# Products of the gradient one unit later in a sliding-window attention backward, and projections in other PSUM banks

## The chip, the cores and the metric

One core of a Trainium2 chip runs one program that computes a forward pass and all its gradients. The metric is the device time of one execution in microseconds (us). The five engines each work through a list of their own in the order in which the program wrote it: TensorE (PE, matrix products and transposes, its weight loads shown as PEld), VectorE (DVE), ScalarE (ACT), GpSimd (POOL) and SyncE (SP), which here only issues DMA transfers. They wait for each other through semaphores.

## The reference

S = 2048 rows, D = 512, 32 heads of Dh = 16, a window of W = 256 keys, F = 1376. Two branches are mixed by a gate per row; the outputs are the mix and the gradients of `A_x`, of both weights of the attention, of the three weights of the feed-forward part and of `gate_w`.

```python
qkv = (x @ wqkv).reshape(B, S, 3, H, Dh).transpose(2, 0, 3, 1, 4)
scores = einsum("bhqd,bhkd->bhqk", q, k) * Dh ** -0.5      # keys 0..255 behind the query only
p = softmax(scores); a = (p @ v).reshape(B, S, D) @ wo
gate = x @ W_gate; up = x @ W_up; b = (gate * (gate > 0) * up) @ W_down
g = sigmoid((x * gate_w).sum(-1, keepdims=True))
out = g * a + (1 - g) * b                                  # and its vjp with grad_out
```

Both branches read the same x, `A_x`.

## The kernel before

There are three stages. **The first** (about 0 to 250 us) computes the feed-forward hidden layer and its gradients in 44 steps, one per block of 128 hidden columns and group of 512 rows; a loop over step numbers `n` (lines 439 to 498) runs eight steps longer than there are steps, so that the delayed parts come out, and in those last steps it also makes the projections of the attention's first group. **The second** (about 250 to 720 us) is the attention, forward and backward, and is where the change lies. **The third** (to the end) reads the spilled gradients back and computes the output and `dx`.

The attention is written as 360 *units*. A unit is one block of 128 queries against one block of 128 keys, for four heads: `c` (0 to 3) is a set of eight heads, `j` (0 to 15) the query block, `kb` = j, j-1 or j-2 the key block (roles "d" for diagonal, "m" for middle, "f" for far), `half` which four of the eight heads. A query block with its full window thus has six units. The while loop from line 875 writes one *slot* per unit, with the parts of several units in it; which part of which unit falls in which slot sets the order of work on every engine. In slot n:

- `front` of unit n (line 666): the scores ST on TensorE (line 672), their exponential on ScalarE (line 682), and for roles d and f the mask on GpSimd (lines 684, 687);
- `gradp` of unit n-1 (line 698): VectorE multiplies the exponentials Pu by the product dPT, which gives Pd. This is "the product" below;
- `flip` of unit n-2 by a DMA transpose, for units that are turned that way;
- `rowsum` of unit n-3 (line 703, `LAG` = 3): four pairs of small matmuls into the bank BA, the first of a pair with Pu (line 710), the second with Pd (line 712). Units of role f, and some of role m, are then turned by eight transposes on TensorE into a bank `pt` and copied out by ScalarE and VectorE in turn (line 734);
- `front_dp` of unit n (line 690): dPT, the gradient of the probabilities, on TensorE (line 696). In the first slot after a finished query block it stands ahead of `rowsum`;
- then pieces that fill the slot: CD (lines 533, 536), the gradients of keys and values; one *part* of the projections of the next group of four query blocks (`project_parts`, line 118); or a quarter of a weight gradient (`grad_parts`, line 613), whose tile is held over four such pieces. A planner counts a `credit` of TensorE time per slot to decide, with a due time per group.

A group (c, four query blocks) has six parts, in order: Q and dO (a matmul chain of four, an evacuation to zT by VectorE), the DMA transpose `tr_rows`, K and V (a matmul chain of four, an evacuation KT or VT by ScalarE, then two masked copies K0, K1 or V0, V1 by VectorE, line 161), and `tr_kv` (eight transposes, two copies on VectorE). After Q and dO of group g+1, four copies called `spread` on VectorE (line 514), one a slot, put them in place.

PSUM has eight banks. In this stage four have the tag M and take ST, dPT, the projections' pp and the weight gradients' wps; two have the tag TR and take the transposes pt and ptp; one is BA, one CD. A tile that finds no free bank of its tag waits for the reader of the one that it is given.

Of the kernel before, what the change touches and what calls it, by code (L numbers as in the profile page):

```python
# [11 lines left out]
BF = mybir.dt.bfloat16  # L12
F32 = mybir.dt.float32
# [9 lines left out]
def kernel(  # L23
# [20 lines left out]
    nc = tc.nc  # L44
    P = 128
# [10 lines left out]
    DC = D // P  # L56
# [55 lines left out]
    if True:  # L112
        HH = HG // 2
        proj = {}
        groups = [(c, tg) for c in range(DC) for tg in range(NTG)]
        PENG = ("dvs", "dvs")

        def project_parts(c, tg):
            t4 = {}
            proj[(c, tg)] = t4  # L120
            pj = pjA if (c * NTG + tg) % 3 == 0 else pjs["b"]

            def mm(nm, which, eng):
                ps, tag, bufs, _, _ = pools["now"]
                pp = ps.tile([P, TGW], F32, tag=tag, bufs=bufs, name="pp")
                for cd in range(DC):
                    if which < 3:
                        nc.tensor.matmul(pp[:], lhsT=w_p[c][:, cd, which * P:(which + 1) * P], rhs=x_T[tg][:, cd, :],  # L128
                                         start=(cd == 0), stop=(cd == DC - 1))
                    else:  # L130
                        nc.tensor.matmul(pp[:], lhsT=w_p[c][:, cd, 3 * P:4 * P], rhs=da_T[tg][:, cd, :],
                                         start=(cd == 0), stop=(cd == DC - 1))
                if nm in ("Q", "dO"):
                    if nm == "Q":
                        t4["z"] = pjA.tile([P, 2, TGW], BF, tag="zT", name="zT")
                    dst = t4["z"][:, ("Q", "dO").index(nm), :]
                else:
                    dst = pjA.tile([P, TGW], BF, tag="T", bufs=2, name=f"{nm}T")[:]
                if nm == "Q" and (c, tg) == groups[1]:
                    nc.scalar.mul(dst, pp[:], scale)  # L140
                elif nm == "Q":
                    nc.vector.tensor_scalar(dst, pp[:], scale, None, op0=ALU.mult)
                else:
                    evac(dst, pp[:], eng)
                t4[nm] = dst
                if nm in ("Q", "dO"):
                    if c == 0 and tg == 0:
                        w = ("Q", "dO").index(nm)
                        for k in range(NP):
                            rows = slice(32 * k, 32 * k + 32)  # L150
                            evac(zt[0][rows, w, k, :, :], dst[rows, :].rearrange("p (k q) -> p k q", k=TPG),
                                 (("dve", "act")[w] if k % 2 else "dve"))
                else:
                    for k in range(2):
                        t4[f"{nm}{k}"] = pj.tile([P, TGW], BF, tag=f"{nm}{k}", name=f"{nm}{k}")
                        if PENG[k] == "act":
                            nc.scalar.mul(t4[f"{nm}{k}"][:], pp[:], par[:, k:k + 1])
                        elif PENG[k] == "dve":
                            nc.vector.tensor_scalar(t4[f"{nm}{k}"][:], pp[:], par[:, k:k + 1], None, op0=ALU.mult)
                        else:  # L160
                            nc.vector.tensor_scalar(t4[f"{nm}{k}"][:], dst[:], par[:, k:k + 1], None, op0=ALU.mult)

            def tr(a_nm, b_nm):
                _, _, _, ps, trt = pools["now"]
                pt = ps.tile([P, 2, TPG, P], BF, tag=trt, bufs=2, name="ptp")
                for a, nm in enumerate((a_nm, b_nm)):
                    for k in range(TPG):
                        nc.tensor.transpose(pt[:, a, k, :], t4[nm][:, k * P:(k + 1) * P], ident[:])
                return pt

            def tr_rows():
                rows = pjA.tile([P, 2, TPG, P], BF, tag="rows", bufs=2, name="rows")
                nc.sync.dma_start_transpose(out=rows[:].rearrange("p a t d -> p (a t) d"),
                                            in_=t4["z"][:].rearrange("p a s -> p (a s)"))
                t4["rows"] = rows

            def tr_kv():
                kv = pj.tile([P, TPG, HG, 34], BF, tag="KV1", name="KV1")
                nc.gpsimd.memset(kv[:, :, :, 0:1], -1.0)
                nc.gpsimd.memset(kv[:, :, :, Dh + 1:Dh + 2], 1.0)  # L180
                pt = tr("K", "V")
                v = lambda a: pt[:, a, :, :].rearrange("p k (h d) -> p k h d", h=HG)
                nc.vector.tensor_scalar(kv[:, :, :, 1:1 + Dh], v(0), scale, None, op0=ALU.mult)
                nc.vector.tensor_copy(kv[:, :, :, Dh + 2:2 * Dh + 2], v(1))
                t4["kv"] = kv

            return [lambda: mm("Q", 0, "dve"), lambda: mm("dO", 3, "dve"), tr_rows, lambda: mm("K", 1, "act"),
                    lambda: mm("V", 2, "act"), tr_kv]

    with ExitStack() as p1, tc.manual_schedule():  # L190
# [248 lines left out]
        for n in range(N1 + 8):  # L439
# [51 lines left out]
            for _ in range({N1 + 1: 2, N1 + 2: 0}.get(n, 1)):  # L491
                if first:
                    first.pop(0)()
            z = n - DA0 - NT - 2
            if z == 0:
                load_w(0)
# [4 lines left out]
    if True:  # L501
# [6 lines left out]
        ps = pps.enter_context(tc.tile_pool(name="attps", bufs=2, space=PSUM))  # L508
        ppr = ExitStack()
        psr = ppr.enter_context(tc.tile_pool(name="attpr", bufs=2, space=PSUM, side="right"))  # L510
        pools["now"] = (ps, "M", 4, psr, "TR")
        def spread(gi, k):
            rows = slice(32 * k, 32 * k + 32)
            nc.vector.tensor_copy(zt[gi % ZB][rows, :, k, :, :].rearrange("p w t q -> p w (t q)"),
                                  proj[groups[gi]]["z"][rows, :, :])

        P2 = {}
        RQ = {}
        CDs = {}
# [93 lines left out]
        def grad_parts(c, tail=False):  # L613
# [6 lines left out]

            def piece(part, t0, first, last):
                if first:
                    hold[part] = ps.tile([P, 3, P], F32, tag="M", bufs=4, name="wps")
                wps = hold[part]
                for t in range(t0, t0 + 4):
                    nc.tensor.matmul(wps[:], lhsT=x_r[:, t, part * P:(part + 1) * P], rhs=sts[c][:, t, 0:3, :],  # L626
                                     start=first and t == t0, stop=last and t == t0 + 3)
                if not last:
                    return None
                ws = (S2["t6"] if tail else gwp).tile([P, 3, P], BF, tag="ws", bufs=5 if tail else 2, name="ws")  # L630
                evac(ws[:], wps[:], "act" if not tail or part % 2 else "dve")
                return store(part, ws)
# [33 lines left out]
        def front(u):  # L666
# [5 lines left out]
            nc.tensor.matmul(ST[:], lhsT=KTt[:, ksl], rhs=z[:, 0, :, jl, :], start=True, stop=True)  # L672
            if not u.own:
                if u.half == 0:
                    kind = "m" if u.c == DC - 1 and u.j > 11 and u.j % 2 == 0 else u.role
                    tag = f"PP{kind}"
                    pairs[(u.c, u.j, u.kb)] = wk.tile([P, 2, 2, HH, P], BF, tag=tag, bufs=3, name=tag)
                u.PP = pairs[(u.c, u.j, u.kb)][:, u.half, :, :, :]
# [42 lines left out]
        def flip(u):  # L721
# [3 lines left out]
            if u.dma:  # L725
# [5 lines left out]
                for b in range(2)[hs]:  # L731
                    P2[(u.c, u.j, u.kb, b)] = P2[key][:, b, :, :, :]
                return
            eng = ("act", "dve")[copier["i"] % 2]
            copier["i"] += 1
            pt = psr.tile([P, 2, HH, P], BF, tag="TR", name="pt")
            for a, src in enumerate((u.Pu, u.Pd)):
# [99 lines left out]
        with tc.manual_schedule():  # L837
# [37 lines left out]
            while n <= NU + LAG or ev or cdq or bgq:  # L875
                now = ev.pop(n, [])
                u = units[n] if n < NU else None
                if u is not None:
# [2 lines left out]
                        sts[u.c] = st.tile([P, NT, 4, P], BF, tag="rows_st", name="rows_st")  # L881
                    if u.first and u.j % TPG == 0:
                        if gi + 1 < len(groups):
                            prq = project_parts(*groups[gi + 1])
                            due = n + sum(2 * min(3, j + 1) for j in range(u.j, u.j + TPG)) - 3
                            if gi + 2 == len(groups):
                                due -= 10
# [9 lines left out]
                for eng, f in now:  # L897
                    if eng == "pool":
                        f()
                if 1 <= n <= NU:  # L900
                    gradp(units[n - 1])
                for eng, f in now:
                    if eng == "dve":
                        f()
                for eng, f in now:
                    if eng == "pool+":
                        f()
                if 2 <= n < NU + 2 and units[n - 2].dma:
                    flip(units[n - 2])
                w = units[n - LAG] if LAG <= n < NU + LAG else None  # L910
                if u is not None and w is not None and w.first:
                    front_dp(u)
                    pieces()
                if w is not None:
                    rowsum(w)
# [2 lines left out]
                    if w.last:  # L918
# [5 lines left out]
                        for kb in done:  # L924
                            qbs = range(kb, min(NT, kb + 3))
                            for qb in qbs:
                                for half in range(2):
                                    e = n + (1 if qb < w.j else 5)
                                    cdq.append((e, w.c, kb, qb, half, qb == qbs[-1] and half == 1))
                if u is not None and not (w is not None and w.first):  # L930
                    front_dp(u)
                credit += SLOT - 0.63 - (0.44 if LAG <= n < NU + LAG and not units[n - LAG].dma else 0.0)
                if not (u is not None and w is not None and w.first):
                    pieces()
                if n >= NU:
                    if bgq:
# [23 lines left out]
                if late and (u is None or u.c == 0 or (n % 12 == 1 and 3 <= u.j <= 8 if u.c < DC - 1 else  # L960
                                                       n % 4 == 1 and 1 < u.j < 10 or n % 2 and u.j > 9)):
                    late.pop(0)()
                if early and n % 3 == 0 and (len(early) > 4 or u is None or u.j >= 11):
                    early.pop(0)()
                credit = max(-1.0, min(1.2, credit))
                for eng, f in now:
# [154 lines left out]
```

## Time and profile before

| what | value |
|---|---|
| median of three runs | 921.34 us (919.93 to 921.94) |
| profiled execution: its own time, its span | 921.62 us, 919.9 us |
| granted TensorE clock, mean | 0.998 |
| TensorE busy | 903.5 us, 98% |
| VectorE, ScalarE, GpSimd busy | 511.5, 437.8, 493.6 us |
| from 270 to 720 us (450 us): TensorE, VectorE, ScalarE, GpSimd busy | 443.37, 341.60, 320.82, 325.55 us |
| scores ST, dPT, products on VectorE | 360 each |

Times of lines are in us from the start of the span. A row of the timeline gives start, duration, engine, line, operation and tiles, and in brackets the idle time of the engine before it and what ended it. Rows of the same kind that follow each other are merged, with their number at the end. A matmul's end in a row is modelled and lies after the start of the next one, so TensorE's share of busy time hides gaps of up to a few tenths; they are read from starts. Records of neighbouring VectorE instructions overlap by a little under a tenth too.

### The profile page before, as it was taken

How to read it: one execution, taken by the hardware profiler on the slowest of the kernel's cores; microseconds unless marked ns; L12 is line 12 of the kernel's file. 1: busy time of each engine (PE TensorE's matmuls, PEld its weight loads, DVE VectorE, ACT ScalarE, POOL GpSimd, SP SyncE). 2: the span in 40 equal slices, each digit the busy share in tenths (PEclk: the TensorE clock that was granted, in tenths of full speed). 3: DMA queues.
4: the chain of work that ended last, by engine and by line, in shares of the span. 5: the costliest groups of instructions: out<-in, count | busy, mean ns of one | idle time of the engine just before them, and what ended most of it. 6: DMA issues, size and time to landing. Idle time of an engine off the chain costs nothing.

```text
span 919.9 us, 26221 instructions
## 1 busy us (share of the span) xinstructions
PE 903.5 (98%) x10711; PEld 569.7 (62%) x10711; DVE 511.5 (56%) x957; ACT 437.8 (48%) x773; POOL 493.6 (54%) x937
## 2 busy tenths in 40 slices
PE   9999999999999999999999999999998999999998
PEld 6556656556657776667666677766776644444445
DVE  4333344334288887668876687777786222222223
ACT  7322222222367777667776677766687300011111
POOL 4544445445277777767787677775777311111111
PEclk9999999999999999999999999999999999999999
DMA  9988889999699999998999989999999799777741
GB/s 303 193 195 188 190 179 215 221 222 194 159 164 157 179 182 187 191 164 149 171 196 187 162 158 182 184 179 185 181 187 197 184 255 234 183 188 184 184 93 46
DMA packets 505576, 169.07 MB, mean 184 GB/s; under 512 B 433456, under 2 KB 504336, under 8 KB 505456
## 3 DMA queue, kind: packets, MB, share of 16 engines
q1 hardware_dynamic: 484816, 145.51, 85.8%
q10 hardware_dynamic: 19008, 17.31, 6.9%
q0 software_dynamic: 1632, 4.59, 1.4%
q8 instruction: 83, 1.36, 0.6%
q14 instruction: 37, 0.30, 0.1%
HBM read 32.28 MB, written 36.24 MB: 74 GB/s over the span
## 4 chain that ended last, share of the span: by engine, by line
PE 79%; POOL 7%; DVE 4%; DMA 4%; issue 2%; ACT 2%; SPq 1%; ACTq 0%; POOLq 0%; DVEq 0%
PE dxps L1046 8%; PE ST L672 7%; PE dPT L696 7%; PE wps L403 7%; PE pt L739 5%; PE wps L626 4%; PE dxps L1050 4%; PE bps L1019 4%; PE pp L128 4%; PE CD L533 3%; PE BA L710 3%; PE dps L405 3%; PE ups L354 3%; PE gps L354 3%; PE dhps L354 3%
## 5 line engine op out<-in xcount | busy, mean ns | idle before, releaser
L696 PE MATMUL dPT<-z,V 128*128 128x512 bf16 x360 | 136.4, 379 | 3.7 <-ACT PPm L682 2.4
L672 PE MATMUL ST<-z,K 128*128 128x512 bf16 x360 | 136.3, 379 | 2.0 <-ACT PPm L682 0.3
L684 POOL TENSOR_SCALAR_AFFINE_SELECT PPd<-PPd 128x512 bf16<-128x512 bf16 x124 | 79.1, 638 | 106.9 <-ACT PPd L682 106.1
L701 DVE TENSOR_TENSOR Pd<-Pu,dPT 128x512 bf16<-128x512 bf16 x117 | 80.1, 684 | 64.7 <-POOL Pu L687 62.7
L368 POOL TENSOR_TENSOR hT<-rg,upm 128x512 bf16<-128x512 bf16 x44 | 51.5, 1171 | 116.1 <-DVE upm L366 90.0
L403 PE MATMUL wps<-dgu_r,x_r 128*128 128x256 bf16 (+1 forms) x704 | 103.9, 270 | 0.9 <-DVE wst L74 0.8
L701 DVE TENSOR_TENSOR PPd<-PPd,dPT 128x512 bf16<-128x512 bf16 x124 | 84.4, 680 | 15.5 <-POOL PPd L684 14.8
L403 PEld LDWEIGHTS <-x_r 128*128 128x128 bf16 x704 | 68.3, 98 | 31.9 <-issue 1.8
L682 ACT ACTIVATE PPd<-ST 128x512 bf16<-128x512 f32 x124 | 74.4, 600 | 27.3 <-PE ST L672 26.5
L682 ACT ACTIVATE PPm<-ST 128x512 bf16<-128x512 f32 x119 | 71.2, 601 | 29.9 <-PE ST L672 25.8
L682 ACT ACTIVATE Pu<-ST 128x512 bf16<-128x512 f32 x117 | 70.2, 600 | 28.9 <-PE ST L672 28.8
L701 DVE TENSOR_TENSOR PPm<-PPm,dPT 128x512 bf16<-128x512 bf16 x119 | 79.4, 667 | 6.5 <-POOL PPm L684 4.1
L687 POOL TENSOR_SCALAR_AFFINE_SELECT Pu<-Pu 128x512 bf16<-128x512 bf16 x112 | 73.7, 658 | 16.2 <-ACT Pu L682 15.6
L1026 ACT COPY a_sb<-aps 128x512 f32<-128x512 f32 x16 | 9.4, 586 | 151.4 <-issue 137.6
L366 DVE SCALAR_TENSOR_TENSOR upm<-rg,ups 128x512 bf16<-128x512 bf16 x44 | 30.1, 684 | 80.6 <-PE ups L354 44.2
L360 ACT ACTIVATE rg<-gps 128x512 bf16<-128x512 f32 x44 | 26.3, 598 | 88.4 <-PE gps L354 33.1
L405 PE MATMUL dps<-db_r,h_r 128*128 128x512 bf16 x176 | 66.7, 379 | 0.0
L72 ACT COPY p<-pt 128x1024 bf16<-128x1024 bf16 x62 | 63.0, 1016 | 5.2 <-PE dPT L696 0.4
L378 POOL TENSOR_TENSOR dgu<-dh_sb,rg 128x512 bf16<-128x512 bf16 x44 | 57.2, 1301 | 5.1 <-ACT dh_sb L374 5.1
L1032 POOL DMA_DIRECT2D out_dram<-o_sb x16 | 8.7, 542 | 89.2 <-DVE o_sb L1030 82.7
L128 PE MATMUL pp<-x,p 128*128 128x512 bf16 x192 | 49.0, 378 | 1.5 <-ACT PPm L682 1.0
L626 PE MATMUL wps<-rows_st,x_r 128*128 128x384 bf16 x256 | 50.3, 325 | 0.0
(193 smaller groups left out, 2362.3 us busy)
## 6 DMA issues: line engine op xcount, KB each, us to landing
dqkvo_d<-rows_st SPq DMA_DIRECT2D x15, 512.0 KB, 4.2
hT_d<-hT ACTq DMA_DIRECT2D x44, 128.0 KB, 2.5
dgT_d<-dgu ACTq DMA_DIRECT2D x44, 128.0 KB, 3.0
duT_d<-dgu ACTq DMA_DIRECT2D x44, 128.0 KB, 3.0
duT_g<-duT_d SPq DMA_DIRECT2D x8, 640.0 KB, 5.6
gt<-hT_d SPq DMA_DIRECT2D x7, 640.0 KB, 6.0
dgT_g<-dgT_d SPq DMA_DIRECT2D x7, 640.0 KB, 5.3
out_dram<-wst SPq DMA_DIRECT2D x20, 128.0 KB, 2.7
```

The lines of the kernel that those rows point to most:

```text
L128: nc.tensor.matmul(pp[:], lhsT=w_p[c][:, cd, which * P:(which + 1) * P], rhs=x_T[tg][:, cd, :], start=(cd == 0), stop=(cd == DC - 1))
L354: nc.tensor.matmul(out[:], lhsT=w(c), rhs=x(c), start=(c == 0), stop=(c == DC - 1))
L403: nc.tensor.matmul(acc["w"][:, c, 0:2 * nw], lhsT=x_r[:, t, c * P:(c + 1) * P], rhs=k.dgu_r[:, :, i, s0:P], start=(go_ and c % 2 == 0), st ...
L405: nc.tensor.matmul(acc["d"][:], lhsT=k.h_r[:, i, :], rhs=db_r[:, t, :], start=go_, stop=no_)
L626: nc.tensor.matmul(wps[:], lhsT=x_r[:, t, part * P:(part + 1) * P], rhs=sts[c][:, t, 0:3, :], start=first and t == t0, stop=last and t == ...
L672: nc.tensor.matmul(ST[:], lhsT=KTt[:, ksl], rhs=z[:, 0, :, jl, :], start=True, stop=True)
L682: nc.scalar.activation(u.Pu[:], ST[:], ACT.Exp)
L684: nc.gpsimd.affine_select(out=u.Pu[:], in_=u.Pu[:], compare_op=ALU.is_ge, fill=0.0, base=0, pattern=[[0, HH], [1, P]], channel_multiplier=-1)
L687: nc.gpsimd.affine_select(out=u.Pu[:], in_=u.Pu[:], compare_op=ALU.is_ge, fill=0.0, base=-1, pattern=[[0, HH], [-1, P]], channel_multiplier=1)
L696: nc.tensor.matmul(u.dPT[:], lhsT=VTt[:, ksl], rhs=z[:, 1, :, jl, :], start=True, stop=True)
L701: nc.vector.tensor_tensor(out=u.Pd[:], in0=u.Pu[:], in1=u.dPT[:], op=ALU.mult)
L1046: nc.tensor.matmul(to, lhsT=src[:, fc, lsl], rhs=W6[(wt, fc)][:, cols], start=(fc == 0 and wt == "Wg"), stop=False)
```

## The change

In the attention's loop, `gradp` in slot n takes unit n-2 where it took n-1, `front_dp` takes unit n-1 where it took n, and the DMA `flip` takes unit n-3 where it took n-2. `front` (unit n) and `rowsum` (unit n-3) stay where they are, as does everything else in the slot: the evacuations of parts, the `spread` copies, the CD pieces.

The projections' tiles pp move from the four M banks to the two TR banks, and so do the weight gradients' tiles wps of the head sets c = 0 and 1, which run while c = 1 and 2 are at work.

Q, dO and `tr_rows` of the second group are made in the last steps of the first stage (steps N1+4 to N1+6), in that stage's banks, with the four `spread` copies right behind dO. The attention's first group then has only K, V and `tr_kv` to make for the second.

Smaller: while c = 0, two of three TensorE-turned units are copied out by ScalarE instead of one of two. In c = 3 the diagonal units share the middle units' buffers at j = 12 only, not at 12 and 14. The transposed loads of the third stage's first group (`early`) start at other slots: the four DMAs from j = 14 on, every second slot, instead of from j = 11 on, every third.

```diff
--- before.py
+++ after.py
@@ -115,10 +115,15 @@
         groups = [(c, tg) for c in range(DC) for tg in range(NTG)]
         PENG = ("dvs", "dvs")
 
+        def spread(gi, k):
+            rows = slice(32 * k, 32 * k + 32)
+            nc.vector.tensor_copy(zt[gi % ZB][rows, :, k, :, :].rearrange("p w t q -> p w (t q)"),
+                                  proj[groups[gi]]["z"][rows, :, :])
+
         def project_parts(c, tg):
             t4 = {}
             proj[(c, tg)] = t4
-            pj = pjA if (c * NTG + tg) % 3 == 0 else pjs["b"]
+            pj = lambda: pjA if (c * NTG + tg) % 3 == 0 else pjs["b"]
 
             def mm(nm, which, eng):
                 ps, tag, bufs, _, _ = pools["now"]
@@ -150,9 +155,12 @@
                             rows = slice(32 * k, 32 * k + 32)
                             evac(zt[0][rows, w, k, :, :], dst[rows, :].rearrange("p (k q) -> p k q", k=TPG),
                                  (("dve", "act")[w] if k % 2 else "dve"))
+                    elif nm == "dO" and (c, tg) == groups[1]:
+                        for k in range(NP):
+                            spread(1, k)
                 else:
                     for k in range(2):
-                        t4[f"{nm}{k}"] = pj.tile([P, TGW], BF, tag=f"{nm}{k}", name=f"{nm}{k}")
+                        t4[f"{nm}{k}"] = pj().tile([P, TGW], BF, tag=f"{nm}{k}", name=f"{nm}{k}")
                         if PENG[k] == "act":
                             nc.scalar.mul(t4[f"{nm}{k}"][:], pp[:], par[:, k:k + 1])
                         elif PENG[k] == "dve":
@@ -175,7 +183,7 @@
                 t4["rows"] = rows
 
             def tr_kv():
-                kv = pj.tile([P, TPG, HG, 34], BF, tag="KV1", name="KV1")
+                kv = pj().tile([P, TPG, HG, 34], BF, tag="KV1", name="KV1")
                 nc.gpsimd.memset(kv[:, :, :, 0:1], -1.0)
                 nc.gpsimd.memset(kv[:, :, :, Dh + 1:Dh + 2], 1.0)
                 pt = tr("K", "V")
@@ -491,6 +499,10 @@
             for _ in range({N1 + 1: 2, N1 + 2: 0}.get(n, 1)):
                 if first:
                     first.pop(0)()
+            if n == N1 + 3:
+                second = project_parts(*groups[1])
+            if n in (N1 + 4, N1 + 5, N1 + 6):
+                second.pop(0)()
             z = n - DA0 - NT - 2
             if z == 0:
                 load_w(0)
@@ -508,12 +520,7 @@
         ps = pps.enter_context(tc.tile_pool(name="attps", bufs=2, space=PSUM))
         ppr = ExitStack()
         psr = ppr.enter_context(tc.tile_pool(name="attpr", bufs=2, space=PSUM, side="right"))
-        pools["now"] = (ps, "M", 4, psr, "TR")
-        def spread(gi, k):
-            rows = slice(32 * k, 32 * k + 32)
-            nc.vector.tensor_copy(zt[gi % ZB][rows, :, k, :, :].rearrange("p w t q -> p w (t q)"),
-                                  proj[groups[gi]]["z"][rows, :, :])
-
+        pools["now"] = (psr, "TR", 2, psr, "TR")
         P2 = {}
         RQ = {}
         CDs = {}
@@ -620,7 +627,8 @@
 
             def piece(part, t0, first, last):
                 if first:
-                    hold[part] = ps.tile([P, 3, P], F32, tag="M", bufs=4, name="wps")
+                    own, tag, bufs = (ps, "M", 4) if c + 2 >= DC else (psr, "TR", 2)
+                    hold[part] = own.tile([P, 3, P], F32, tag=tag, bufs=bufs, name="wps")
                 wps = hold[part]
                 for t in range(t0, t0 + 4):
                     nc.tensor.matmul(wps[:], lhsT=x_r[:, t, part * P:(part + 1) * P], rhs=sts[c][:, t, 0:3, :],
@@ -672,7 +680,7 @@
             nc.tensor.matmul(ST[:], lhsT=KTt[:, ksl], rhs=z[:, 0, :, jl, :], start=True, stop=True)
             if not u.own:
                 if u.half == 0:
-                    kind = "m" if u.c == DC - 1 and u.j > 11 and u.j % 2 == 0 else u.role
+                    kind = "m" if u.c == DC - 1 and u.j == 12 else u.role
                     tag = f"PP{kind}"
                     pairs[(u.c, u.j, u.kb)] = wk.tile([P, 2, 2, HH, P], BF, tag=tag, bufs=3, name=tag)
                 u.PP = pairs[(u.c, u.j, u.kb)][:, u.half, :, :, :]
@@ -731,7 +739,7 @@
                 for b in range(2)[hs]:
                     P2[(u.c, u.j, u.kb, b)] = P2[key][:, b, :, :, :]
                 return
-            eng = ("act", "dve")[copier["i"] % 2]
+            eng = ("act", "dve", "act")[copier["i"] % 3] if u.c == 0 else ("act", "dve")[copier["i"] % 2]
             copier["i"] += 1
             pt = psr.tile([P, 2, HH, P], BF, tag="TR", name="pt")
             for a, src in enumerate((u.Pu, u.Pd)):
@@ -881,7 +889,7 @@
                         sts[u.c] = st.tile([P, NT, 4, P], BF, tag="rows_st", name="rows_st")
                     if u.first and u.j % TPG == 0:
                         if gi + 1 < len(groups):
-                            prq = project_parts(*groups[gi + 1])
+                            prq = project_parts(*groups[gi + 1]) if gi else second
                             due = n + sum(2 * min(3, j + 1) for j in range(u.j, u.j + TPG)) - 3
                             if gi + 2 == len(groups):
                                 due -= 10
@@ -897,19 +905,20 @@
                 for eng, f in now:
                     if eng == "pool":
                         f()
-                if 1 <= n <= NU:
-                    gradp(units[n - 1])
+                if 2 <= n <= NU + 1:
+                    gradp(units[n - 2])
                 for eng, f in now:
                     if eng == "dve":
                         f()
                 for eng, f in now:
                     if eng == "pool+":
                         f()
-                if 2 <= n < NU + 2 and units[n - 2].dma:
-                    flip(units[n - 2])
                 w = units[n - LAG] if LAG <= n < NU + LAG else None
-                if u is not None and w is not None and w.first:
-                    front_dp(u)
+                v = units[n - 1] if 1 <= n <= NU else None
+                if w is not None and w.dma:
+                    flip(w)
+                if v is not None and w is not None and w.first:
+                    front_dp(v)
                     pieces()
                 if w is not None:
                     rowsum(w)
@@ -927,10 +936,10 @@
                                 for half in range(2):
                                     e = n + (1 if qb < w.j else 5)
                                     cdq.append((e, w.c, kb, qb, half, qb == qbs[-1] and half == 1))
-                if u is not None and not (w is not None and w.first):
-                    front_dp(u)
+                if v is not None and not (w is not None and w.first):
+                    front_dp(v)
                 credit += SLOT - 0.63 - (0.44 if LAG <= n < NU + LAG and not units[n - LAG].dma else 0.0)
-                if not (u is not None and w is not None and w.first):
+                if not (v is not None and w is not None and w.first):
                     pieces()
                 if n >= NU:
                     if bgq:
@@ -960,7 +969,7 @@
                 if late and (u is None or u.c == 0 or (n % 12 == 1 and 3 <= u.j <= 8 if u.c < DC - 1 else
                                                        n % 4 == 1 and 1 < u.j < 10 or n % 2 and u.j > 9)):
                     late.pop(0)()
-                if early and n % 3 == 0 and (len(early) > 4 or u is None or u.j >= 11):
+                if early and (u is None or n % 2 == 0 and u.j >= (9 if len(early) > 4 else 14)):
                     early.pop(0)()
                 credit = max(-1.0, min(1.2, credit))
                 for eng, f in now:
```

## The prediction

> **What bounds the kernel now.** I read the page's busy times first, then what TensorE and VectorE waited for, then the timeline where the change acts.
>
> ```profile
> PE 903.5 (98%) x10711; PEld 569.7 (62%) x10711; DVE 511.5 (56%) x957; ACT 437.8 (48%) x773; POOL 493.6 (54%) x937
> ```
> ```profile
> PE dPT L696 <- ACT PPm L682: 2.4, 1, 2.4
> ```
> ```profile
> DVE Pd L701 <- POOL Pu L687: 62.7, 81, 1.5
> DVE PPd L701 <- POOL PPd L684: 14.8, 20, 1.7
> ```
>
> TensorE is the bound, and it is nearly full. VectorE idles 77 us before products because GpSimd's masks come late, but hardly any of that reaches TensorE. As matmul ends are modelled, I measured TensorE's gaps by starts: 512 columns take 0.216 us back to back, 128 columns 0.055 us, the smallest 0.025 us; what a start is later than that is a gap. From 249 to 719 us there are 119 gaps over 0.04 us, 23.1 us together; those over 0.12 us make 18.3 us. That is all that the change can win, so the question is what new waits it makes. They show at a projection's K, here for group c=1, j=12 to 15. TensorE, ScalarE, VectorE:
>
> ```profile
> 426.59 0.38 PE L672 MATMUL ST<-z,K 128*128 128x512 bf16 x1
> ...
> 427.70 0.38 PE L672 MATMUL ST<-z,K 128*128 128x512 bf16 x1
> 427.91 0.18 PE L710 MATMUL BA<-KV,Pu 128*128 128x33 bf16 x1
> 427.94 0.17 PE L712 MATMUL BA<-KV,Pd 128*128 128x17 bf16 x1
> ```
> ```profile
> 426.79 0.59 ACT L72 CAST KT<-pp 128x512 bf16<-128x512 f32 x1 [1.03 <-PE pp L128]
> ```
> ```profile
> 425.37 0.43 DVE L514 COPY z<-zT 32x1024 bf16<-32x1024 bf16 x1
> 426.34 0.69 DVE L701 TENSOR_TENSOR Pd<-Pu,dPT 128x512 bf16<-128x512 bf16 x1 [0.53 <-POOL Pu L687]
> 427.06 0.63 DVE L514 COPY z<-zT 32x1024 bf16<-32x1024 bf16 x1
> 427.70 1.04 DVE L161 TENSOR_SCALAR K<-KT,par 128x512 bf16<-128x512 bf16 x2
> 428.66 0.67 DVE L701 TENSOR_TENSOR PPm<-PPm,dPT 128x512 bf16<-128x512 bf16 x1
> 429.26 0.67 DVE L701 TENSOR_TENSOR Pd<-Pu,dPT 128x512 bf16<-128x512 bf16 x1
> ```
>
> K's matmuls end a slot at 426.59. ScalarE copies KT until 427.38, and VectorE, in order, makes K0 and K1 until 428.74 and only then starts the next product. The matmul of BA at 427.94 needs the product that began at 426.34, ended 0.91 us before: it stands ahead of K0 and K1 in VectorE's list.
>
> **The products (the main term).** After the change, the place in VectorE's list where product k stood holds product k-1, while `rowsum` stays where it was. So the place at 428.66, behind K0 and K1, holds the product that the matmul at 427.94 waits for. If nothing else moved, it would end at 429.33, 1.39 us late. Something does move: the 0.53 us wait for the mask at 426.34 ends, K0 can start when KT is there (427.40), and the product ends at about 429.0, still 1.1 us late. The chain from the end of K's matmuls is 0.2 (latency) + 0.6 (KT) + 0.9 (K0, K1) + 0.7 (product) = 2.4 us; TensorE reaches that `rowsum` after one slot, a ST and one small matmul, 1.35 us. Before there was one more slot (1.30 us on average) to cover it.
>
> Queued behind a late product are all the products after it; behind the waiting `rowsum` on TensorE stand the flip, dPT and the next ST, so the time is lost whole. To sum it I went down VectorE's rows from 249.5 to 720 us: each starts when the one before is done (record less 0.08 us, the overlap of neighbouring records) and its input is there (the producer's time in this trace, plus TensorE's shift so far); each product is put one place later; where it ends after its BA matmul of this trace, the difference joins the shift. With the products in their own places this gives a shift of 0.01 us, so the method invents none. One place later it gives 48.8 us:
>
> - behind K0, K1: 14 places, 13.4 us; behind V0, V1: 12, 11.6 us
> - behind `tr_kv`'s two copies: 14, 8.7 us
> - behind Q's evacuation: 14, 4.0; behind dO's: 13, 4.3; behind spread alone: 8, 2.4 us
> - behind a flip's copy on VectorE: 26, 4.4 us
>
> With an overlap of 0.06 or 0.10 us it is 52.2 or 45.4 us.
>
> **What is won.** A product no longer waits for a mask of its own slot's unit, and TensorE, when it waits at `rowsum`, gives the others time; I take all gaps over 0.12 us as gone: -18.3 us. Among them is the largest, at 701.85 to 704.60, where an exponential had no buffer because the shared PPm buffers were waiting for a DMA; j=14's diagonal units now have a buffer of their own. But a gap taken out brings TensorE to the same `rowsum` earlier, and the same walk without those gaps gives 53.4 us. Net +35.1. Bounds: no gap of before goes (+48.8), or every gap over 0.04 goes (55.9 - 23.1 = +32.8). I take the middle one because most gaps over 0.12 stand at pp waiting for an M bank or behind masks, both of which the change touches.
>
> **Q and dO of group 1 moved.** Eight matmuls, 8 x 0.216 = 1.7 us of TensorE in either place: nothing. Q's copy (ScalarE, 0.60), dO's (VectorE, 0.69), four spreads (1.85) and the DMA transpose (SP 1.84) fall where ScalarE idles from 243.4 to 249.8, VectorE from 246.4 to 250.3 and SP from 243.5 to 250.3; without that cover their 0.6 and 2.5 us would delay the first exponential and the first product. Without them the walk is 0.7 us shorter in the first group: -0.7. The gaps of 250 to 268 us make 4.0 (already in the 18.3), but 1.7 us of filling work is gone there too: between -1.7 and +1.7 around my value.
>
> **Projections and wps in TR.** The waits of pp for an M bank (16 gaps after dPT, 1.7; 23 after CD, 0.7) are in the sum above. New ones: a pp or flip waits for the copy of the flip before last, at most 1.02 us (ScalarE, pt). Flips are two or four slots apart (2.6 us or more), so with two banks the older is free: 0. While one of the eight wps tiles holds a bank, a flip waits for the one two slots back: 0.44 + 0.3 + 1.02 against 2.6 us: 0, at most 0.3 for some 16 flips, 5 us. I take 0.
>
> **The small edits.** Copier at c=0: five of 28 copies move from VectorE (0.68) to ScalarE (1.02), which is busy three quarters of the time there; -1 to +1, taken as 0. DMA flips one slot later: CD is due at least one query block after all but the last; buffers PPd and PPm have three copies; 0, up to +2 at the end. The early loads leave SP at j=11 to 13 and join four Wd loads from j=14; T0 is wanted after 733, some 15 us later: 0, up to +2.
>
> **Sum** on the profiled execution, 921.62 us (span 919.9; 0.3 above the median 921.34): 921.6 + 53.4 - 18.3 - 0.7 = 956.0 us.
>
> The clock. After the 2.53 us gap at 701.85 the trace grants half the clock from 706.08 to 709.49.
>
> ```profile
> 702.00:704.00 2.00, 0.23 (x2) 0.00 (x0) 0.18 (x1) 0.05 (x1) 0.00 (x0) 1.00 0.53 142
> ...
> 706.00:708.00 2.00, 2.00 (x28) 1.45 (x25) 1.40 (x4) 1.66 (x3) 1.75 (x5) 0.52 0.91 193
> ```
>
> Gaps up to 0.6 us in 250 to 268 left it at 1.00. My waits, up to 1.4 us, lie between, nearer the latter; I add nothing and keep a rival. The Trainium skill (TensorE: Matmul & The Clock Gate, "What's actually happening") says that the clock halves after an idle window of about 3.4 us; the trace's 2.53 us gap was enough. By that rule no wait here would trip it, and the sum stays 956.0.
>
> **Rivals.**
> - *Only K and V bite.* The lateness behind the shorter evacuations is absorbed, as VectorE, no longer waiting for masks, gets ahead. For: 77 us of mask waits end. Against: the walk has taken them out already. 13.4 + 11.6 - 18.3 = +6.7, to +15.4 with `tr_kv`: 928 to 937; with smaller or larger K waits 923 to 948.
> - *Faster.* VectorE's list is not what `rowsum` meets: if the evacuations' places came, on average, a slot before they are needed, only the gaps would go: 921.6 - 18.3 = 903, or 898 with all 23.1. It decides from the point where all new waits together are under 18.3 us, 0.7 us a K or V place and none elsewhere. Against: K's chain, 2.4 us against 1.35, is counted from rows that nothing in the diff shortens.
> - *No change*: waits of 18 us that just replace the old; nothing makes them equal.
> - *The clock trips* at K's waits: half of 3.41 us lost, at most 1.7, at 14 places: 956 + 24 = 980.
>
> **How the numbers follow.** The forecast has 0.66, with a range of its own of 951 (45.4 us, raised by 7.1 and less 23.1) to 971 (no old gap gone). Only K and V: 0.17. Faster: 0.11. Within 0.2% (1.8 us, about what runs spread over 2 us can tell): 0.02. Clock: 0.04. The range of 8 in 10 goes from 928, which takes in most of the second case, to 970. Slower by over 0.2%: 0.66 + 0.17 + 0.04 = 0.87.
>
> **What would show it.** TensorE's list of waits should have BA L712 (or L710) waiting for DVE products, tens of us in some 100 places, in place of 0.8 us; VectorE's 62.7 us for masks should be nearly gone; behind each K0, K1 the matmul of BA should start about 1 us after its ST. The gap near 702 and the drop of the clock should be gone. The first stage should end about 1.7 us later, the third keep its length. I am wrong if BA hardly waits: then VectorE's order, or the slots behind a part, are not as I read them.

## The result and the profile after

The changed kernel takes 957.22 us (957.03 to 957.37, four runs) against 920.63 us beside it: 1.0399 times as long, 95% interval 1.0379 to 1.0419. The profiled execution took 957.03 us, with a span of 955.1 us against 919.9.

The page's busy times of the changed kernel:

```profile
PE 906.8 (95%) x10711; PEld 563.7 (59%) x10711; DVE 509.5 (53%) x952; ACT 442.6 (46%) x778; POOL 498.1 (52%) x937
```

The instructions on TensorE are the same 10711, its busy time is 3 us more, and its share falls from 98 to 95%: the loss is waiting. What TensorE waited for, longest first (total us, times, longest):

```profile
PE BA L720 <- DVE Pd L709: 25.7, 43, 1.4
PE BA L720 <- DVE PPm L709: 5.5, 13, 0.6
PE BA L720 <- DVE PPd L709: 4.8, 9, 0.7
```

Line 720 is the second matmul of `rowsum`'s pair, line 709 the product on VectorE (712 and 701 before). This list leaves out the short waits that a modelled matmul end covers; measured from start to start, TensorE stands 53.2 us between the two matmuls of a pair, at 100 places, against 0.6 us before. On the other side, VectorE's long wait for GpSimd's masks, 62.7 us before, has become this:

```profile
DVE Pd L709 <- POOL Pu L695: 5.5, 8, 0.9
```

The place that the prediction worked through (K of group c=1, j=12 to 15) now looks like this, first on TensorE, then on ScalarE, then on VectorE:

```profile
442.28 0.38 PE L680 MATMUL ST<-z,K 128*128 128x512 bf16 x1
442.49 0.18 PE L718 MATMUL BA<-KV,Pu 128*128 128x33 bf16 x1
443.55 0.18 PE L720 MATMUL BA<-KV,Pd 128*128 128x17 bf16 x1 [0.88 <-DVE Pd L709]
```
```profile
441.44 0.59 ACT L72 CAST KT<-pp 128x512 bf16<-128x512 f32 x1 [0.94 <-PE pp L133]
```
```profile
440.93 0.44 DVE L120 COPY z<-zT 32x1024 bf16<-32x1024 bf16 x1
442.06 0.84 DVE L169 TENSOR_SCALAR K<-KT,par 128x512 bf16<-128x512 bf16 x2 [0.69 <-ACT KT L72]
442.81 0.68 DVE L709 TENSOR_TENSOR Pd<-Pu,dPT 128x512 bf16<-128x512 bf16 x1
```

VectorE sits idle for 0.69 us in front of K0 until ScalarE has made KT, with the product that TensorE needs queued behind K0 and K1; TensorE starts the pair's first matmul at 442.49, and the second starts 1.06 us after the first, where it is 0.03 when nothing is late. Of the 100 late products 89, with 47.4 of the 53.2 us, start directly behind another VectorE instruction (its record touches or overlaps theirs), and 7 more, with 4.5 us, start 0.03 us behind one, their dPT long made. Two, with 0.2 us together, wait for a dPT that had only just been made, and two, with 1.0 us, for a mask.

All gaps over 0.04 us in the attention (first ST to last CD) went from 23.1 to 57.1 us, +34.0, and the attention from 478.9 to 512.7 us, +33.8. Without the waits at BA the gaps fell from 22.5 to 3.9 us. The first ST is 1.5 us later, and TensorE's work from the last CD to its own last matmul takes 187.7 us in both. The attention lost eight matmuls, about 1.8 us, to the first stage; gaps of under 0.04 us, which this count leaves out, grew by 1.5 us and make up for them.

The clock held: it is at full through the whole attention, with waits of up to 1.4 us, and the dip behind the gap at 702 us is gone with that gap. The stretch with the longest wait (its length; PE, PEld, DVE, ACT and POOL busy; then the granted clock, the share of DMA and GB/s):

```profile
470.00:480.00 10.00, 7.78 (x132) 5.02 (x129) 7.86 (x16) 6.04 (x11) 6.13 (x14) 1.00 0.87 160
```

### The profile page after: what moved, and what is told of

Its sections match the earlier page's. It is cut to its first block, busy times and chain, and to the rows that moved or that the text cites. A ratio compares the mean times of both kernels' runs of the same rounds, so it can differ in the third digit from the quotient of the medians.

```text
span 955.1 us, 26227 instructions
## 1 busy us (share of the span) xinstructions
PE 906.8 (95%) x10711; PEld 563.7 (59%) x10711; DVE 509.5 (53%) x952; ACT 442.6 (46%) x778; POOL 498.1 (52%) x937
## 4 chain that ended last, share of the span: by engine, by line
PE 77%; DVE 10%; issue 4%; ACT 3%; DMA 2%; POOL 2%; SPq 1%; DVEq 0%; ACTq 0%; POOLq 0%
PE dxps L1055 7%; PE wps L411 7%; PE dPT L704 6%; PE pt L747 6%; PE ST L680 5%; PE pp L133 4%; PE wps L634 4%; PE dxps L1059 4%; DVE Pd L709 4%; PE bps L1028 4%; PE BA L720 3%; PE dps L413 3%; PE ups L362 3%; PE BA L718 3%; PE gps L362 3%
## 5 line engine op out<-in xcount | busy, mean ns | idle before, releaser
L709 DVE TENSOR_TENSOR PPm<-PPm,dPT 128x512 bf16<-128x512 bf16 x117 | 79.7, 682 | 20.0 <-PE dPT L704 18.6
L72 ACT COPY p<-pt 128x1024 bf16<-128x1024 bf16 x67 | 68.3, 1019 | 22.5 <-PE pt L747 21.6
L720 PE MATMUL BA<-KV,Pd 128*128 128x17 bf16 x468 | 38.6, 172 | 27.9 <-DVE Pd L709 25.7
L720 PEld LDWEIGHTS <-Pd 128*128 128x128 bf16 x468 | 28.6, 96 | 52.8 <-DVE Pd L709 47.3
```

The lines of the kernel that those rows point to most:

```text
L72: nc.scalar.copy(out, in_)
L709: nc.vector.tensor_tensor(out=u.Pd[:], in0=u.Pu[:], in1=u.dPT[:], op=ALU.mult)
L720: nc.tensor.matmul(BA[:, h, 33:50], lhsT=u.Pd[:, hh, :], rhs=kv[:, u.kb % TPG, h, 0:17], start=False, stop=True, skip_group_check=True)
```

## The experiments

Theory A: the product stands one place later on VectorE, behind the evacuations of the projections, and TensorE waits for it in `rowsum`. Rival B: the loss comes from the two TR banks and the other parts. Rival C: the product is late because its input dPT is made a slot later. The ratio after each time is against the kernel before on the same chip.

**The products' part alone, on the kernel before.**

```diff
-                if 1 <= n <= NU:
-                    gradp(units[n - 1])
+                if 2 <= n <= NU + 1:
+                    gradp(units[n - 2])
...
+                v = units[n - 1] if 1 <= n <= NU else None
+                if w is not None and w.dma:
+                    flip(w)
...
-                    front_dp(u)
+                    front_dp(v)
```

> The kernel before with the products' part of the change alone: gradp takes unit n-2, front_dp unit n-1, the DMA flip unit n-3; projections stay in the M banks, Q and dO of group 1 in the attention, nothing else touched. Theory A (each product stands one place later on VectorE, behind the evacuations, and rowsum waits for it): 48.8 us of new waits at BA, less the mask-bound gaps of before (some 5 us), so about 965 us (955 to 972), BA waiting for VectorE some 50 us. Rival B (the loss comes from projections and weight gradients in the two TR banks and the moved parts): within 5 us of before, 916 to 926.

Measured 962.51 us, 1.0452 (1.0418 to 1.0486). TensorE's waits:

```profile
PE BA L712 <- DVE Pd L701: 24.4, 43, 1.1
PE BA L712 <- DVE PPm L701: 5.3, 13, 0.6
PE BA L712 <- DVE PPd L701: 4.9, 9, 0.9
PE dPT L696 <- ACT PPm L682: 2.7, 1, 2.7
```

The three rows at BA are those of the changed kernel within 1.3 us; from start to start BA waits 52.8 us. The part alone makes more than the whole loss, with projections in the M banks: B falls. The time lies within the range of A, 2.5 us under its middle. The gaps outside BA's pairs fell from 22.5 to 9.0 us here too, though no bank was changed. The gap near the end (fourth row) stays, as buffers and loads were not touched.

**Everything but the products' part.** The same lines the other way round, on the changed kernel.

> The changed kernel with the products' part undone: gradp takes unit n-1, front_dp unit n, the DMA flip unit n-2; TR banks, moved Q and dO, buffers, copier and early loads as changed. Theory A: no waits at BA, and what the other parts win of the 23 us of gaps shows: the gap near 702 with its half clock (3 us) and the waits of pp for M banks (some 4 us), so about 913 us (905 to 920). Rival B: about 950 us.

Measured 912.66 us, 0.9926 (0.9897 to 0.9955): 0.7% under the kernel before. Gaps of the attention are 14.9 us, and what is left at BA's second matmul is this row:

```profile
PE BA L720 <- DVE Pd L709: 0.4, 1, 0.4
```

The parts add up to within 2 us: +42.3 for the products and -7.6 for the rest make +34.7, and both together measured +36.6. With the products late the rest is worth less: it takes the ratio from 1.0452 to 1.0399, about 4.9 us.

**K, V and tr_kv's copies behind the next product.** On the changed kernel, only VectorE's order is altered; dPT, banks and slots stay.

```diff
+        later = []
+        def soon(f):
+            later.append(f) if pools.get("defer") else f()
...
-                            nc.vector.tensor_scalar(t4[f"{nm}{k}"][:], dst[:], par[:, k:k + 1], None, op0=ALU.mult)
+                            soon(lambda o=t4[f"{nm}{k}"], k=k: nc.vector.tensor_scalar(
+                                o[:], dst[:], par[:, k:k + 1], None, op0=ALU.mult))
...
+                    pools["defer"] = True
                     prq.pop(0)()
+                    pools["defer"] = False
+                    for f in later:
+                        ev.setdefault(n + 1, []).append(("dve", f))
+                    later.clear()
```

> The changed kernel, but K0, K1, V0, V1 and tr_kv's two copies are written into VectorE's list one slot later, behind the next product instead of ahead of it. Theory A: the waits at BA that stand behind these (K 11.6, V 12.5, tr_kv 7.7 us) mostly go, some 5 us come back where the copies push the product after: about 932 us (925 to 940). Rival C (the product is late because dPT, its input, comes a slot later than before, whatever stands ahead of it): no change, 952 to 960.

Measured 926.27 us, 1.0064 (1.0044 to 1.0084), some 31 us less than the changed kernel. VectorE at the same K, and TensorE's waits:

```profile
429.29 0.44 DVE L124 COPY z<-zT 32x1024 bf16<-32x1024 bf16 x1
429.76 0.69 DVE L714 TENSOR_TENSOR Pd<-Pu,dPT 128x512 bf16<-128x512 bf16 x1
430.42 0.84 DVE L173 TENSOR_SCALAR K<-KT,par 128x512 bf16<-128x512 bf16 x2
```
```profile
PE BA L725 <- DVE Pd L714: 5.9, 17, 0.7
PE BA L725 <- DVE PPd L714: 1.9, 4, 0.6
PE BA L725 <- DVE PPm L714: 1.8, 4, 0.6
```

The product now goes first, and when it is done K0 finds KT ready. BA's waits from start to start, sorted by what stands between the late product and the one before it on VectorE:

| behind | predicted (walk of 48.8) | changed kernel | copies deferred |
|---|---|---|---|
| K0, K1 | 13.4 | 11.6 (14 places) | 0 |
| V0, V1 | 11.6 | 12.5 (12) | 0.2 |
| tr_kv's copies | 8.7 | 7.7 (13) | 1.7 |
| Q, dO | 4.0, 4.3 | 4.3, 5.9 (28) | 4.3, 5.9 |
| flip's copy, spread | 4.4, 2.4 | 6.6, 3.4 (29) | 5.2, 3.5 |
| others | 0 | 1.2 (4) | 1.4 |
| sum | 48.8 | 53.2 | 22.2 |

The three kinds that were moved lose 29.9 of 31.8 us, and those that were not stay as they were. dPT is still made a slot later, so C falls for these kinds; the 5 us that I expected to come back did not. For Q, dO, flips and spread, 20.2 of the 53.2 us, the order was not altered: that they delay products in the same way rests on what stands directly ahead of the product, and on the runs with a later `rowsum` below.

**dPT a slot earlier.** One line of the changed kernel.

```diff
-                v = units[n - 1] if 1 <= n <= NU else None
+                v = u
```

> The changed kernel with front_dp back at unit n, so that dPT is there a slot before the product is due; the product stays at unit n-2. Theory A (the product is late because of what stands ahead of it on VectorE): BA waits as in the changed kernel, some 40 us in c = 0 to 2 against 43, time about 958 us (953 to 970; two dPT are alive at a time, so ST waits more often for a bank, above all in c = 3). Rival C (late because dPT comes a slot later): BA's waits go, under 925 us.

Measured 963.44 us, 1.0471 (1.045 to 1.0492). The time is A's, but what makes it is not what A said: while c = 0 to 2 are at work, BA waits 23.1 us, where 40 were expected, and 29.5 us in all. With two dPT alive, ST waits for banks instead (23 us more before ST, at places where no record is missing). That VectorE catches up during these waits is likely, but not shown.

```profile
PE BA L720 <- DVE Pd L709: 10.5, 29, 0.8
PE ST L680 <- ACT PPm L690: 3.7, 11, 0.4
```

It shows that an earlier dPT wins no time here; it does not by itself tell A from C, which the deferred copies did.

**rowsum one slot later as well (LAG 4)**, in three forms. The first needed room for third buffers of Pu and Pd and took it from PPd:

```diff
-            LAG = 3
+            LAG = 4
...
-wk.tile([P, 2, 2, HH, P], BF, tag=tag, bufs=3, name=tag)
+wk.tile([P, 2, 2, HH, P], BF, tag=tag, bufs=2 if kind == "d" else 3, name=tag)
...
```

> The changed kernel with rowsum one slot later too (LAG 4), so that a product has again two slots before it is needed; three buffers instead of two for Pu and Pd, and to make room two instead of three for PPd. Theory A: the 53 us at BA fall under 5, time about 907 us (900 to 915). Rival B: BA's wait moves but the time stays over 940 us. If two PPd buffers are too few, ScalarE waits for a DMA now and then and the time lies up to 10 us higher.

Measured 952.94 us, 1.0358 (1.0322 to 1.0394), a miss. BA waits for no product in TensorE's list any more (0.6 us from start to start), but ScalarE now waits for the third PPd buffer, far more than the 10 us that I allowed:

```profile
ACT PPd L690 <- DMA p2d<-PPd: 52.0, 21, 6.0
```

The second form keeps three PPd buffers; the middle units of c=3, half 1, stay in their pair's buffer instead.

```diff
-                        u.own = u.role == "f" or (u.role == "m" and half == 1 and not u.pair and j < 10)
+                        u.own = u.role == "f"
```

> The changed kernel with rowsum one slot later (LAG 4) and three PPd buffers as before; room for it comes from letting the middle units of c=3, half 1, use their pair's buffer, so that Pu and Pd need no third buffer. Theory A: BA's waits fall from 53 to under 6 us and nothing takes their place: about 905 us (899 to 913), below the 912.7 us of the run without the products' part. Rival D (what the two-buffer run showed: with rowsum so late, buffers come free too late whatever their number): over 930 us.

Measured 918.37 us, 0.9974 (0.9955 to 0.9992): BA's waits for products are down to 0.5 us, as A says, and D, which stood for over 930 us, falls; but the time missed A's 905. At the very end CD waits for the last diagonal unit's DMA, which SP issued behind two others at 718 us, and the clock halves behind that. TensorE's row, and the stretches 720 to 725 and 725 to 730:

```profile
PE CD L540 <- DMA p2d<-PPd: 4.3, 1, 4.3
```
```profile
720.00:725.00 5.00, 0.71 (x27) 0.62 (x24) 0.00 (x0) 0.37 (x1) 0.00 (x0) 0.64 1.04 162
725.00:730.00 5.00, 5.00 (x26) 2.47 (x23) 1.79 (x6) 1.33 (x3) 0.96 (x1) 0.68 0.76 209
```

The third form turns that last unit pair on TensorE:

```diff
-                        u.pair = u.role == "d" or
+                        u.pair = (u.role == "d" and not (c == DC - 1 and j == NT - 1)) or
...
```

> LAG 4 with three PPd buffers, and the last diagonal units (c=3, j=15) turned on TensorE instead of by a DMA. In the LAG 4 run CD waited 4.4 us for that DMA at the end, and the clock fell behind it. If that is what LAG 4 loses against the run without the products' part: CD's wait goes, eight transposes and some 0.9 us of TensorE come, about 912.5 us (910 to 915). If LAG 4 loses elsewhere: 916 to 920.

Measured 912.3 us, 0.9915 (0.9902 to 0.9929), as expected. So the products can go two slots behind if `rowsum` follows, but that is then no better than products one slot behind with everything else of the change.

**The other parts.** Without the products' part, projections and wps back in the M banks:

```diff
-        pools["now"] = (psr, "TR", 2, psr, "TR")
+        pools["now"] = (ps, "M", 4, psr, "TR")
...
-                    own, tag, bufs = (ps, "M", 4) if c + 2 >= DC else (psr, "TR", 2)
+                    own, tag, bufs = ps, "M", 4
```

> The run without the products' part, but projections and weight gradients back in the M banks: what is left of the change is the moved Q and dO, the buffers, the copier and the early loads. If the TR banks win the waits of pp and dPT for M banks (some 4 us), about 917 us; if the banks do nothing, 912.7 us; if TR costs, under 911 us.

Measured 921.77 us, 1.0011 (0.9998 to 1.0024). The TR banks are worth about 8 us (0.9926 against 1.0011), twice what I expected: besides pp's own waits (2.6 us after dPT), the waits of ST and dPT for banks shrink (ST after BA 4.0 to 2.6, dPT after BA 3.6 to 2.6, after ST 2.6 to 1.9), perhaps because pp no longer shifts whose bank comes next, which no run shows. That is with the products in their old place; with the products late, pp's waits are nearly gone with M banks too (0.3 us in the run with the products' part alone), and a gain from the banks there is not shown. The gaps make 23.1 us against 14.9. (Some projection records are missing in this trace, and gaps of 0.2 us at their places are not counted.)

The kernel before with the buffers at j=12 alone and the early loads' slots:

```diff
-                    kind = "m" if u.c == DC - 1 and u.j > 11 and u.j % 2 == 0 else u.role
+                    kind = "m" if u.c == DC - 1 and u.j == 12 else u.role
...
-                if early and n % 3 == 0 and (len(early) > 4 or u is None or u.j >= 11):
+                if early and (u is None or n % 2 == 0 and u.j >= (9 if len(early) > 4 else 14)):
```

> The kernel before with only the shared buffers of the diagonal units (at j=12 alone) and the slots of the early loads changed. The gap of 2.5 us at 702 and the half clock behind it go: about 917.5 us (916.5 to 918.5), granted clock 1.00 from 700 to 720. If the gap is only moved: 920 us, as before.

Measured 918.2 us, 0.9988 (0.9971 to 1.0004). The wait of dPT near 702 and the half clock are gone from the trace; the time is the expected one, though its interval just reaches no change.

Without the products' part, and with Q and dO of group 1 back in the attention:

```diff
...
-            if n == N1 + 3:
-                second = project_parts(*groups[1])
-            if n in (N1 + 4, N1 + 5, N1 + 6):
-                second.pop(0)()
...
-                            prq = project_parts(*groups[gi + 1]) if gi else second
+                            prq = project_parts(*groups[gi + 1])
```

> The run without the products' part, and also with Q, dO and the row transposes of group 1 back in the attention (in the TR banks): what is left of the change is the TR banks, the buffers, the copier and the early loads. The run without the products' part shows the first ST waiting 0.9 us for VectorE's copy of dO, which the prediction had at nothing. If the move costs that wait and the filling work it takes from the attention's start: 910 us (909 to 911.5). If the move is worth 0.7 us as predicted: 913.4 us.

Measured 912.43 us, 0.9911 (0.9898 to 0.9925), against 0.9926 with the move: no difference that these runs can tell. Neither expectation was right. The attention starts 1.3 us earlier and is 1.4 us longer.

## Why the prediction was right

The forecast was 956.0 us, 1.2 us below the median, and both of its larger terms came out near their size. That the total is as close as 1.2 us is partly luck. The kernel before spreads over 3 us in the runs beside the changed one; the profiled run of before waits 2.0 us on TensorE near 30 us, in code of the first stage that the change leaves alone, and the changed kernel's 0.5 us; and the forecast left out the gaps of under 0.04 us, which grew by 1.5 us.

- **New waits at BA.** 53.4 us predicted, 53.2 measured, at the places that were named. The split by kind was given for the walk with the old gaps in, 48.8 us; against it (the table above) K came out 2 us lower, where VectorE's masked copies are a little shorter now (0.84 us for the two in the place shown, 1.04 before), and dO, flips and spreads 1 to 2 us higher each. The single place was predicted 1.1 us late; it was 1.03. That the delay is VectorE's order, and not the later dPT, the deferred copies showed for K, V and `tr_kv`, 31.8 of the 53.2 us.
- **Gaps that go.** 18.3 us predicted, 22.5 - 3.9 = 18.6 us measured. The size is partly luck: the prediction let the gaps of over 0.12 us go and the smaller ones stay (4.8 us); what the trace shows outside BA's pairs is that the smaller ones went too (0.1 us left) and that 3.8 us of gaps over 0.12 stand, seven of them in front of CD. The reason was right at 702 us. Of the others, TensorE's own waiting, which gives the other engines time, is enough to explain the most: with the products' part alone, in the M banks, 9.0 us remain outside BA's pairs (2.9 of them the gap near the end), and with everything but that part 14.9 us in all.
- **Q and dO moved.** -0.7 us predicted; the run without the products' part shows no gain. The step that failed is that all but TensorE's 1.7 us, which the sum had as neutral, falls where the engines are idle: the first ST now waits for the bank that dO's copy empties (0.9 us in the list of waits), which the prediction had not seen. The first ST stands at 250.4 to 253.8 us in the eight traces with the move and at 248.8 to 250.1 us in the four without.
- **TR banks.** No new wait at 0 was right: pp waits nowhere over 0.04 us in the changed kernel, where it had waited 3.2 us. What the banks win was in the sum as the waits of pp alone (2.4 us); with the products in their old place it is about 8 us.
- **Small edits.** 0 for early loads and copier: the third stage has the same 187.7 us. The copier was not tried alone. Between the run with M banks (921.77 us) and the one with only buffers and loads (918.20 us) lie 3.6 us. They should come from the copier or from the move of Q and dO. Their traces point to the first stage and so away from the copier: the attention is 476.9 us long against 476.2, and the first ST stands at 253.5 us against 248.8. In part that is the wait on TensorE near 30 us, 1.95 us in the one and 0.81 in the other, which also differs between kernels with the same code there. It is one trace of each, and the cause stays open.
- **Rivals.** Only K and V: the shorter evacuations make 21.4 us of the 53.2 (all but K and V 29.1), so they are not absorbed. Faster: the waits passed the deciding 18.3 us threefold. Clock: not tripped by waits up to 1.4 us, though these runs do not show how much room was left: in the first form of LAG 4 it fell at 270.9 us behind waits of 1.30, 0.27 and 0.70 us within three microseconds. The Trainium skill (TensorE: Matmul & The Clock Gate, "What's actually happening") gives an idle window of about 3.4 us before the clock halves; the changed kernel's short waits and the second LAG 4 form's 4.4 us gap agree with it, the 2.53 us gap of the kernel before and the waits just named do not.

## What to carry to other kernels

Where an engine works in order, a step moved back in its list does not only start later: it lands behind whatever was written between the two places, and behind what that waits for. Before shifting a stage of a software pipeline, measure for each consumer how long before its use the input is ready; here the median margin of a product was 1.03 us, one slot is 1.30 us, and the chain from K's last matmul to the end of the product behind it takes 2.4. The margin alone does not say which products will be late: 221 of the 360 had less than a slot of it, and 100 were late, nearly all of them those with other work written between the two places. So walk the list itself. An engine's idle time (77 us of VectorE here) is no reason to shift if the bound engine hardly waits for it; shift the consumer too, or put the slow evacuation behind the urgent instruction, which won back 31 of the 36.6 us here.

## What the runs showed of the hardware

- The length of one TensorE gap did not decide whether the clock fell to half. It fell behind single gaps of 2.53 us (kernel before, half clock from 706.08 to 709.49), 2.91 us (products' part alone, 744.53 to 747.94) and 4.43 us (second form of LAG 4), and not behind gaps of 2.63 and 2.85 us in the first form of LAG 4. In that form it also fell behind waits of 1.30, 0.27 and 0.70 us that followed each other within three microseconds. It did not fall around the changed kernel's longest wait of 1.4 us, with TensorE idle for 2.2 of 10 us (470 to 480 us). The stretch ahead of the fall behind the short waits, and the one behind it, in the first form of LAG 4:

```profile
267.50:270.90 3.40, 1.61 (x28) 1.01 (x28) 2.66 (x5) 2.13 (x5) 2.80 (x8) 1.00 1.22 259
270.90:274.30 3.40, 3.40 (x41) 2.13 (x38) 0.76 (x2) 2.15 (x3) 3.11 (x8) 0.50 0.75 140
```

- Between the first two forms with LAG 4 lie 35 us. In the first, with two PPd buffers, ScalarE waited 52.0 us in total for the turn by DMA, which takes 5.4 us from issue to landing in the kernel before, though a buffer is needed only every six slots (7.8 us); in the second, with three, it has no such wait. The forms differ in the buffers of Pu and Pd and of c = 3 as well, which were not tried apart.
